# 16-bit lo squares from the third superblock on, in a convolution and squared-ReLU MLP kernel

## The chip, the cores and the metric

One core of one Trainium2 chip runs the kernel. The metric is the device time of one execution in microseconds (us), the median of several runs.

## What is computed

From the reference, cut:

```
# a causal convolution of 7 taps over the sequence, softmax taps, one set per head
w = exp(weight - max) / (sum + 1e-9)                  # 8 heads x 7 taps
out[b, s, h] = sum over k of w[h, k] * x[b, s + k - 6, h]   # x: 8 x 4096 x 192
# and a layer over its 32768 tokens of 192 channels
h = out @ w_in                                        # 192 x 2048
r = max(h, 0)
g = s * r * r + b
y = g @ w_out                                         # 2048 x 192
```

All inputs are 32-bit floats; the two weight matrices arrive as 64-bit words and each is kept as a hi and a lo part.

## The kernel before

Tokens lie along the free dimension. A superblock n is 1024 tokens (32 of them, NSUP), in two blocks j of 512; the 2048 hidden features are 8 pairs p of 256 (NPAIR). One **step** (n, j, p) is `first` (L702), the 18 matmuls of half height that give h for one pair; then on ScalarE `relu` and `square`; then the square is split into a hi part qh (a cast to fp32r, on ScalarE or VectorE) and a lo part ql = q - qh on VectorE; and `second` (L844), which multiplies qh by w_out's hi and lo parts and ql by w_out's hi part and adds into the block's accumulators. `second` runs two steps behind `first` (LAG, L28; three at a block's first pair), from a queue.

The lo part comes in two kinds, and SCALED (L34) says where the one gives way to the other. For superblocks n < SCALED, `lows` (L742) makes ql in 32 bits, and `second` runs 8 more half matmuls in each step for it (L854, operand ql). For n >= SCALED, `half_lows` (L769) makes ql in 16 bits into a ring of 26 places; the A columns of w_out (128 of the 192) are multiplied by all 8 pairs' ql at the block's end (L881), and the B columns (the other 64) for a batch of three blocks in one go (`lows_B`, L828), the earlier ones held until then (`holds`, L841). 16 bits need values of a known size, so for these superblocks the taps and weights are scaled by powers of two:
- `peak` (L227): VectorE finds the largest input of a superblock, SyncE's queue sends it to DRAM and reads it back to all partitions (`to_all`, L168). `scale` (L236) makes the scaled taps from it.
- `weight_tops` (L633): the maxima of the weights, a pair a step, during (SCALED - 1, 0); then `weight_peaks` (L645) sends them by POOL's queue to DRAM and back; `weight_scales` (L651) at (SCALED - 1, 1, 2) makes the scales.
- `halve` (L665): 16-bit copies of w_out in (SCALED, 0); `rescale` (L677): ScalarE scales w_out in place over 8 steps from (SCALED - 1, 1, 4) on.

`column_sums` (L608) adds up w_out over the hidden features, for the b term of g: on VectorE, a pair a step in (1, 1), and the four folds of the last lines at its end. `biases` (L686) uses them in (2, 0, 0).

The convolution of superblock n + 1 runs on VectorE beside the matmuls of n, in small parts: `convolve(k)` (L1003) draws k parts from the generator `Tokens.steps` (L340) of the next superblock. For superblock 1 (`steps_begin`, L345) these are 7 taps of A for block 0, 2 parts of its split, 7 taps of B, 2 parts of its split, 7 taps of A for block 1, 2 parts of its split. For later ones (`steps_by_block`, L355): 7 taps of B, a cast, then for each block 7 taps of A, the split of B, and two parts of the split of A: a copy on ScalarE, and the subtraction on VectorE, after which SyncE's queue issues the two swap DMAs of wA (L271, L272), a copy of sA with its halves exchanged. So a later superblock's first block is ready to use after 18 parts. A convolution's last tap ends a call early, except at p = 1, and what is left over is owed to the next call. BEGIN (L45) and PARTS (L39) say how many parts a step draws. `first` reads sA, then tB and wB, then wA.

What sets the order: each engine runs its own list of instructions in order, and so does each DMA queue (SyncE's SP queue, POOL's queue). The lists are made at build time by a scheduler that goes by the order of the code and by what is ready; `behind(engine)` (L140) keeps an instruction behind the last one of that engine in the code, `headed` (L1087) behind the head's last SyncE instruction, and the first superblock is kept in the order of the code (`in_order`, L144).

Of the kernel before, what the change touches and what calls it, by code (L numbers as in the profile page):

```python
# [9 lines left out]
F32 = mybir.dt.float32  # L10
# [8 lines left out]
P = 128  # L19
# [11 lines left out]
GAP = 128  # L31


SCALED = 3  # L34

RING = 26

# [5 lines left out]
)  # L43

BEGIN = {  # L45
    (1, 0): (3,) * 8,
    (1, 1): (1,) * 8,
# [4 lines left out]
}  # L52


# [8 lines left out]
def conv_attention_then_squared_relu_mlp(  # L63
# [137 lines left out]
    class Tokens:  # L201
# [34 lines left out]
        def scale(self):  # L236

            m = greatest(self.peaks, 1)
            v = small.tile([P, 3], F32, name="v", bufs=4)
            powers(m, v[:, 0:1], v[:, 1:2], -40)  # L240
            taps = small.tile([P, 2, K], F32, name="taps")
            nc.vector.tensor_scalar(
                taps, tap, v[:, 1:2], 2.0**3 if self.n == SCALED else c8,
                op0=ALU.mult, op1=ALU.mult,
            )
            self.tapA, self.tapB = taps[:, 0, :], taps[:, 1, :]
            self.v = v

        def unscale(self):

# [224 lines left out]
    def fetch(p, a=0, z=None):  # L475
        if a == 0:
            words[p] = wordp.tile([P, CT, 2], I32, name="words")
        z = z or CT
        nc.sync.dma_start(
            words[p][:, a:z].rearrange("p f w -> p (f w)"), w_words[p, :, 2 * a : 2 * z]  # L480
        )
# [126 lines left out]
    def column_sums(k):  # L608

        nonlocal sumA, sumB  # L610
        if k == 1:
            free = wordp.tile([P, CT, 2], I32, name="words").bitcast(F32)
            free = free.rearrange("p f w -> p (f w)")
            sumA = free[:, 0 : 4 * P].rearrange("p (h c) -> p h c", h=2)
            sumB = free[:, 4 * P : 4 * P + 5 * DB]
            nc.gpsimd.memset(sumB[:, 0:DB], 0.0)
        for o, w in (
            (sumA, W[:, k, :, CI:CB]),
            (sumB[:, DB:].rearrange("p (j d) -> p j d", j=2), WB[:, k, :, :]),
        ):  # L620
            before = W[:, 0, :, CI:CB] if o is sumA else WB[:, 0, :, :]
            before = before.bitcast(F32) if k == 1 else o
            nc.vector.tensor_tensor(o, before, w.bitcast(F32), op=ALU.add)
        if k == NPAIR - 1:
            a, b = sumA, sumB[:, DB:]
            nc.vector.tensor_tensor(a[:, 0, :], a[:, 0, :], a[:, 1, :], op=ALU.add)
            nc.vector.tensor_tensor(a[:, 0, 0:P], a[:, 0, 0:P], a[:, 0, P:], op=ALU.add)
            nc.vector.tensor_tensor(b[:, 0:P], b[:, 0:P], b[:, P:], op=ALU.add)
            nc.vector.tensor_tensor(b[:, 0:DB], b[:, 0:DB], b[:, DB:P], op=ALU.add)

# [99 lines left out]
    def squares(h, cast, scale=1.0):  # L730
        return square(relu(h, scale), cast)
# [37 lines left out]
    def half_lows(n, j, p, q, qh):  # L769


        k = ((n - SCALED) * 2 + j) * NPAIR + p
        ql = low_halves[n, j, p] = place(k % RING)
        nc.vector.tensor_tensor(  # L774
            ql.rearrange("p f (b a) -> p f b a", a=2),
            *(v.rearrange("p f (a b) -> p f b a", a=2) for v in (q, qh.bitcast(F32))),
            op=ALU.subtract,
        )
        return qh, ql
# [58 lines left out]

    held = []

    def holds(n, j):  # L841
        return n >= SCALED and (n, j) != steps[-1][:2] and (2 * (n - SCALED) + j) % BATCH < BATCH - 1

    def second(n, j, p, qh, ql):  # L844
        if (n, j, p) == steps[-1]:
# [157 lines left out]
    def convolve(k, stops=True):  # L1003


        k += owed[0]
        with behind(nc.vector, nc.scalar):
            while k and coming[0] in tok:
                try:
                    stop = next(tok[coming[0]].todo)  # L1010
                except StopIteration:
                    coming[0] += 1
                    continue
                k -= 1
                if stop and stops:
                    break
        owed[0] = k if coming[0] in tok else 0

    def pair(p):

        ha, hb = first(0, 0, p), first(0, 1, p)
        if p + 1 < NPAIR:
            if p not in TWICE:
                wide[p + 1].rest()
            ahead, between = 0, CONV[p] // 4
        else:
            ahead, between = CONV[p] // 2, CONV[p] // 4
        convolve(ahead)
        def magnitudes():
            if p + 2 < NPAIR:  # L1030
                wide[p + 2].magnitudes()

        if p + 1 in TWICE:
            return ahead_of_two(p, ha, hb, magnitudes)

        qa = relu(ha)
        if p in TWICE:
            qb = relu(hb)
            waiting.pop()()
            magnitudes()  # L1040
        qa = square(qa, nc.scalar.copy)
        if p not in TWICE:
            magnitudes()
        queue.append((0, 0, p, *lows(*qa)))
        if p + 2 < NPAIR:
            wide[p + 2].top()
        convolve(between)
        if p not in TWICE:
            qb = relu(hb)
        qb = square(qb, nc.scalar.copy)  # L1050
        if p + 2 < NPAIR:
            wide[p + 2].his()
        queue.append((0, 1, p, *lows(*qb)))
        convolve(CONV[p] - ahead - between)
# [29 lines left out]
    with in_order(nc.vector, nc.scalar, nc.tensor):  # L1084
        with in_order(nc.sync):
            head()
        headed = last_of(nc.sync)  # L1087
        for p in range(NPAIR):
            if p > 1:
                if p + 3 < NPAIR:  # L1090
                    with headed():
                        fetch(p + 3)
                pair(p)
            if p > 0 and p not in TWICE:
                while len(queue) > (LAG if p < NPAIR - 1 else 0):
                    second_whole(*queue.pop(0))
# [3 lines left out]
    for n, j, p in steps:  # L1100
        if p == 0:
            tok[n].finish(j)
            if j == 0:
                with headed():
                    start_tokens(n + 1)
            else:
                tok.pop(n - 1)
                if n >= SCALED:
                    with behind(nc.vector):
                        tok[n].unscale()  # L1110
                    tok_s[n] = tok[n].s
        if j == 1 and SCALED <= n + 2 < NSUP:
            if p == 0:
                load_tokens(n + 2)
            elif p == 5:
                with behind(nc.vector):
                    ahead[n + 2].peak()
        if n == SCALED - 1:
            if j == 0:
                with behind(nc.vector):  # L1120
                    weight_tops(p)
                    if p == NPAIR - 1:
                        wide_tops = weight_peaks()
            elif p == 2:
                with behind(nc.vector):
                    weight_scales(wide_tops)
        if (n, j) == (SCALED, 0):
            with behind(nc.vector):
                halve(p)
        if (n, j, p) in again:  # L1130
            with behind(nc.scalar):
                rescale(again[n, j, p])
        with begun() if n == 1 else ExitStack():
            h = first(n, j, p)
            if n < SCALED:
                on_scalar = (n, j) in ((1, 0), (2, 0)) or (n, j, p % 2) == (1, 1, 1)
                low = lows(*squares(h, nc.scalar.copy if on_scalar else nc.vector.tensor_copy))
            else:
                low = half_lows(n, j, p, *squares(h, nc.vector.tensor_copy, c if n == SCALED else 1.0))
            queue.append((n, j, p, *low))  # L1140
        if (j, p) == (0, 1) and SCALED <= n + 1 < NSUP:
            with behind(nc.vector):
                tok[n + 1].scale()
        if (n, j) == (1, 1):
            if p < NPAIR - 1:
                with behind(nc.vector):
                    column_sums(p + 1)
        if (n, j) in BEGIN:
            convolve(BEGIN[n, j][p], p != 1)
        else:  # L1150
            batched = (2 * (n - SCALED) + j) % BATCH == 0
            convolve(PARTS[batched][j][p], p != 1)
        if (n, j, p) == (2, 0, 0):
            biases()


        while queue and len(queue) > LAG + (queue[0][2] == 0 and queue[0][:2] != (1, 0)):
            item = queue.pop(0)
            (second if item[0] else second_whole)(*item)
# [47 lines left out]
```

## Time and profile before

| what | value |
|---|---|
| median of 3 runs | 2039.15 us (2037.92 to 2039.29) |
| the profiled execution | 2037.69 us |
| its span, first to last instruction | 2035.9 us |
| granted TensorE clock, mean | 1.000 |
| chain that ended last | TensorE 96%, VectorE 3% |

The span lacks the start and end of the execution, 1.8 us. Busy shares are shares of the span. The matmuls overlap (two of half height run beside each other), so a matmul's own duration says little; the distance from one group's start to the next group's is what it costs.

### The profile page before, as it was taken

The page shows a single profiled execution, that of the slowest core. Times are in us where ns is not written, and L with a number is a line of the kernel's source. Part 1 is how long each engine was busy: PE and PEld are TensorE (multiplying, and loading weights), DVE is VectorE, ACT ScalarE, POOL GpSimd, SP SyncE. Part 2 cuts the span into 40 slices and gives each one's busy share as a digit, 9 for nine tenths or more (in the row PEclk, how much of TensorE's full clock was granted, in tenths as well). Part 3 has the DMA queues.
Part 4 walks back from the last instruction along what each step waited for, and adds up shares of the span by engine and source line. Part 5 has one row for each costly group of instructions (what it writes and reads, how often), then busy time and mean ns, then how long its engine had stood idle before and what let it go on. Part 6 is the DMA issues. An engine that isn't in the chain of part 4 may idle for free.

```text
span 2035.9 us, 43199 instructions
## 1 busy us (share of the span) xinstructions
PE 2026.6 (100%) x18404; PEld 1643.4 (81%) x18404; DVE 1692.0 (83%) x2340; ACT 1324.1 (65%) x1444; POOL 242.5 (12%) x319
## 2 busy tenths in 40 slices
PE   9999999999999999999999999999999999999999
PEld 6889987877878887878778788888787787888886
DVE  9888897888888888878788888878787888888874
ACT  8878766656666565666656666656666666656564
POOL 0001101010110101010101111010101011110101
PEclk9999999999999999999999999999999999999999
DMA  5013333242332332332424323323324243232221
GB/s 197 21 45 92 81 81 80 52 94 60 87 78 68 80 81 66 80 76 55 95 56 91 75 66 84 76 71 76 76 58 97 56 92 73 61 91 66 61 63 40
DMA packets 74625, 152.83 MB, mean 75 GB/s; under 512 B 19040, under 2 KB 23008, under 8 KB 74432
## 3 DMA queue, kind: packets, MB, share of 16 engines
q1 hardware_dynamic: 44448, 86.87, 16.3%
q0 software_dynamic: 29840, 63.07, 14.9%
q8 instruction: 144, 2.36, 0.6%
q14 instruction: 49, 0.40, 0.1%
q10 hardware_dynamic: 144, 0.13, 0.0%
HBM read 35.57 MB, written 25.20 MB: 30 GB/s over the span
## 4 chain that ended last, share of the span: by engine, by line
PE 96%; DVE 3%; issue 0%; DMA 0%; SPq 0%; DVEq 0%
PE h L711 48%; PE acc L854 33%; PE acc L881 10%; PE h L834 3%; PE acc L834 2%; DVE ql L744 1%; DVE c L452 0%; DVE t L438 0%; DVE accA L263 0%; DVE t L435 0%; DVE W L460 0%; DVE W L458 0%; DVE c L451 0%; DVE t L431 0%; PE acc L794 0%
## 5 line engine op out<-in xcount | busy, mean ns | idle before, releaser
L727 ACT ACTIVATE q<-h 128x1024 f32<-128x1024 f32 x492 | 502.7, 1022 | 492.1 <-PE h L711 492.1
L739 DVE CAST qh<-q 128x1024 fp32r<-128x1024 f32 x477 | 330.9, 694 | 288.5 <-ACT q L734 287.5
L734 ACT ACTIVATE q<-q 128x1024 f32<-128x1024 f32 x508 | 539.6, 1062 | 14.1
L854 PE MATMUL acc<-qh,W 64*128 64x512 f32 x3960 | 510.7, 376 | 0.0
L711 PE MATMUL h<-sA,W 64*128 64x512 f32 x3072 | 430.2, 384 | 3.5 <-DVE W L460 1.9
L854 PEld LDWEIGHTS acc<-qh,W 64*128 64x128 f32 x3960 | 379.0, 186 | 50.2
L711 PE MATMUL h<-wA,W 64*128 64x512 f32 x3072 | 417.9, 376 | 0.0
L711 PE MATMUL h<-tB,W 64*128 64x512 f32 x1536 | 413.6, 376 | 0.0
L711 PE MATMUL h<-wB,W 64*128 64x512 f32 x1536 | 413.6, 376 | 0.0
L711 PEld LDWEIGHTS h<-sA,W 64*128 64x128 f32 x3072 | 293.9, 186 | 51.9 <-DVE W L460 2.6
L711 PEld LDWEIGHTS h<-wA,W 64*128 64x128 f32 x3072 | 294.5, 186 | 39.1
L711 PEld LDWEIGHTS h<-tB,W 64*128 64x128 f32 x1536 | 283.7, 186 | 26.0 <-issue 0.2
L854 PE MATMUL acc<-qh,WB 64*128 64x512 f32 x1980 | 297.1, 376 | 0.0
L711 PEld LDWEIGHTS h<-wB,W 64*128 64x128 f32 x1536 | 283.7, 186 | 13.0
L263 DVE SCALAR_TENSOR_TENSOR accA<-xA,taps,accA 128x512 f32<-128x512 f32 x348 | 260.1, 748 | 3.1
L774 DVE TENSOR_TENSOR ql<-q,qh 128x1024 f16<-128x1024 f32 x180 | 226.9, 1261 | 6.2
L854 PEld LDWEIGHTS acc<-qh,WB 64*128 64x128 f32 x1980 | 190.1, 186 | 25.4 <-DVE qh L739 0.4
L774 DVE TENSOR_TENSOR more<-q,qh 128x1024 f16<-128x1024 f32 x140 | 176.5, 1261 | 4.8
L881 PEld LDWEIGHTS <-words 64*128 64x128 f16 x1852 | 85.5, 94 | 113.2 <-issue 17.3
L910 POOL DMA_DIRECT2D oB<-oB x60 | 58.0, 967 | 745.0 <-ACT oB L898 715.4
L774 DVE TENSOR_TENSOR words<-q,qh 128x1024 f16<-128x1024 f32 x108 | 136.2, 1261 | 3.7
L263 DVE SCALAR_TENSOR_TENSOR accB<-xB,taps,accB 128x512 f32<-128x512 f32 x174 | 130.2, 748 | 1.5
(182 smaller groups left out, 1611.4 us busy)
## 6 DMA issues: line engine op xcount, KB each, us to landing
wA<-sA SPq DMA_DIRECT2D x126, 256.0 KB, 4.3
wB<-tB SPq DMA_DIRECT2D x124, 128.0 KB, 2.9
oB<-oB POOLq DMA_DIRECT2D x60, 256.0 KB, 3.5
oA<-oA POOLq DMA_DIRECT2D x60, 256.0 KB, 3.8
outT<-oA POOLq DMA_DIRECT2D x60, 256.0 KB, 2.3
xA<-in_xA SPq DMA_DIRECT2D x24, 515.0 KB, 3.6
xB<-in_xB SPq DMA_DIRECT2D x32, 259.0 KB, 2.6
oB<-oB POOLq DMA_DIRECT2D x60, 128.0 KB, 3.7
```

The costliest lines, as they stand in the source:

```text
L263: nc.vector.scalar_tensor_tensor(acc, src, w[:, k : k + 1], acc, op0=ALU.mult, op1=ALU.add)
L711: nc.tensor.matmul(h[:, i, :], w_in(w, p, chunk[0], rows), folded(chunk[part]), start=start, stop=stop,)
L727: nc.scalar.activation(q, h, AF.Relu, scale=scale)
L734: nc.scalar.activation(q, q, AF.Square)
L739: cast(qh, q)
L744: nc.vector.tensor_tensor(ql, q, qh.bitcast(F32), op=ALU.subtract)
L774: nc.vector.tensor_tensor(ql.rearrange("p f (b a) -> p f b a", a=2), *(v.rearrange("p f (a b) -> p f b a", a=2) for v in (q, qh.bitcast(F3 ...
L834: nc.tensor.matmul(to[k * DB :][0:DB], halves[1][:, 2 * p + k, :], ql[:, k, :], start=start and p == 0, stop=p == NPAIR - 1, skip_group_ch ...
L854: nc.tensor.matmul(accs[to + 2 * i], w(f, r), folded(q[r, f % 2, :]), start=start and f == 0, stop=stop and f == ends[i],)
L881: nc.tensor.matmul(accs[2 * i], halves[0][r, f, :], low[r], start=False, stop=f == ends[i],)
L910: nc.gpsimd.dma_start(o[1], o[3], accum_op=ALU.add)
```

## The change

SCALED goes from 3 to 2: superblock 2 has 16-bit lo squares as well. What hangs on SCALED moves with it: `weight_tops` to (1, 0), `weight_scales` to (1, 1, 2), `rescale` to (1, 1, 4) and on, `halve` to (2, 0). The peak of superblock 2 is taken in (1, 0, 0), its scale in (1, 0, 5), and its convolution can't begin before that (`ready`). `column_sums` becomes DMAs on POOL's queue, the first a copy, the other seven accumulating, a pair a step in (1, 0) by the code; the folds are `fold_sums`, in (1, 1, 3). BEGIN has new numbers. Batches are counted from the end, so the first one is of two blocks. Casts of qh: ScalarE takes all of (1, 0), p < 4 of (1, 1), and p > 4 of (2, 0); VectorE the others.

```diff
-SCALED = 3
+SCALED = 2
 BEGIN = {
-    (1, 0): (3,) * 8,
-    (1, 1): (1,) * 8,
-    (2, 0): (2, 2, 2, 2, 2, 2, 2, 1),
-    (2, 1): (2, 3, 2, 2, 1, 0, 1, 2),
-    (3, 0): (2, 2, 2, 2, 2, 2, 2, 1),
-    (3, 1): (2, 4, 2, 1, 1, 0, 1, 2),
+    (1, 0): (0, 2, 2, 2, 2, 1, 2, 2),
+    (1, 1): (3, 3, 2, 2, 2, 1, 2, 2),
+    (2, 0): (2, 2, 2, 2, 2, 2, 2, 3),
+    (2, 1): (2, 4, 2, 1, 1, 0, 1, 2),
 }
+        def ready(self):
+            return self.n < SCALED or hasattr(self, "v")
     def column_sums(k):
-        if k == 1:
+        if k == 0:
...
+        how = {"accum_op": ALU.add} if k else {}
         for o, w in (
             (sumA, W[:, k, :, CI:CB]),
             (sumB[:, DB:].rearrange("p (j d) -> p j d", j=2), WB[:, k, :, :]),
         ):
-            before = W[:, 0, :, CI:CB] if o is sumA else WB[:, 0, :, :]
-            before = before.bitcast(F32) if k == 1 else o
-            nc.vector.tensor_tensor(o, before, w.bitcast(F32), op=ALU.add)
-        if k == NPAIR - 1:
-            ...
+            nc.gpsimd.dma_start(o, w.bitcast(F32), **how)
+    def fold_sums():
+        ...
+    def left(n, j):
+        return 2 * (NSUP - 1 - n) - j
     def holds(n, j):
-        return n >= SCALED and (n, j) != steps[-1][:2] and (2 * (n - SCALED) + j) % BATCH < BATCH - 1
+        return n >= SCALED and (n, j) != steps[-1][:2] and left(n, j) % BATCH > 0
     # convolve
-            while k and coming[0] in tok:
+            while k and coming[0] in tok and tok[coming[0]].ready():
     # the head's loop over p
+                if p == 5:
+                    with headed():
+                        load_tokens(SCALED)
     # the loop over steps
+        if (n, j, p) == (SCALED - 1, 0, 0):
+            with behind(nc.vector):
+                tok[SCALED].peak()
             if n < SCALED:
-                on_scalar = (n, j) in ((1, 0), (2, 0)) or (n, j, p % 2) == (1, 1, 1)
+                on_scalar = j == 0 or p < 4
...
-                low = half_lows(n, j, p, *squares(h, nc.vector.tensor_copy, c if n == SCALED else 1.0))
+                cast = nc.scalar.copy if (n, j) == (SCALED, 0) and p > 4 else nc.vector.tensor_copy
+                low = half_lows(n, j, p, *squares(h, cast, c if n == SCALED else 1.0))
-        if (j, p) == (0, 1) and SCALED <= n + 1 < NSUP:
+        if (j, p) == (0, 5 if n < SCALED else 1) and SCALED <= n + 1 < NSUP:
             with behind(nc.vector):
                 tok[n + 1].scale()
-        if (n, j) == (1, 1):
-            if p < NPAIR - 1:
-                with behind(nc.vector):
-                    column_sums(p + 1)
+        if (n, j) == (1, 0):
+            column_sums(p)
+        if (n, j, p) == (1, 1, 3):
+            with behind(nc.vector):
+                fold_sums()
-            batched = (2 * (n - SCALED) + j) % BATCH == 0
+            batched = left(n, j) % BATCH == BATCH - 1
```

## Rows read from the trace of the kernel before

A timeline's columns are the start in us, the us from there to the group's end, the engine (SPq is SyncE's DMA queue), the line, the operation, out<-in, the number of instructions merged, and in brackets the idle time before it with what ended it.

**Rows 1.** The page's first part (busy us, share of the span, number of instructions) and the granted clock in 40 slices of the span, in tenths.

```profile
PE 2026.6 (100%) x18404; PEld 1643.4 (81%) x18404; DVE 1692.0 (83%) x2340; ACT 1324.1 (65%) x1444; POOL 242.5 (12%) x319
...
PEclk9999999999999999999999999999999999999999
```

**Rows 2.** What TensorE's matmuls waited for, over the whole span (us in total, times, longest), and the last such wait in TensorE's timeline.

```profile
PE h L711 <- DVE W L460: 1.9, 1, 1.9
...
71.99 0.48 PE L711 MATMUL h<-sA,W 64*128 64x512 f32 x2 [0.19 <-DVE W L466]
```

**Rows 3.** TensorE's timeline in superblock 1: the start of first(1,1,0) and its reading of wA, the start of the next step, the lo squares of second(1,1,2), the start of first(2,0,0), its reading of wB and of wA.

```profile
119.54 0.81 PE L711 MATMUL h<-sA,W 64*128 64x512 f32 x6
...
120.83 0.81 PE L711 MATMUL h<-wA,W 64*128 64x512 f32 x6
...
123.64 0.81 PE L711 MATMUL h<-sA,W 64*128 64x512 f32 x6
...
139.18 0.60 PE L854 MATMUL acc<-ql,WB 64*128 64x512 f32 x4
...
152.34 0.81 PE L711 MATMUL h<-sA,W 64*128 64x512 f32 x6
...
153.64 0.81 PE L711 MATMUL h<-wA,W 64*128 64x512 f32 x6
```

**Rows 4.** TensorE's timeline with 16-bit lo squares: the end of block (3,0) with its A columns' group (L881) and the next step, two successive steps of (3,1), and the first rows of the B columns' groups of the first and the second batch of three blocks (L834).

```profile
252.87 3.63 PE L881 MATMUL acc<-ql,words 64*128 64x512 f16 x32
256.15 1.00 PE L711 MATMUL h<-sA,W 64*128 64x512 f32 x6
...
269.28 0.81 PE L711 MATMUL h<-sA,W 64*128 64x512 f32 x6
...
272.52 0.81 PE L711 MATMUL h<-sA,W 64*128 64x512 f32 x6
...
311.70 2.35 PE L834 MATMUL h<-ql,words 128*64 128x512 f16 x20
...
405.19 0.62 PE L834 MATMUL h<-more,words 128*64 128x512 f16 x4
```

**Rows 5.** VectorE's timeline in (2,0): from the weight maxima of one step to those of the next, with a lo square and two taps between.

```profile
170.52 0.87 DVE L640 TENSOR_REDUCE tops<-W 128x1 f32<-128x384 f32 x2
...
174.09 0.87 DVE L640 TENSOR_REDUCE tops<-W 128x1 f32<-128x384 f32 x2
```

**Rows 6.** The way of the weights' maxima in VectorE's timeline (both_tops; and m, the first instruction of the scales, behind two DMAs on POOL's queue) and POOL's timeline: the memset of the column sums' buffer and the next thing POOL did.

```profile
185.74 0.29 DVE L648 TENSOR_REDUCE both_tops<-tops 128x1 f32<-128x8 f32 x2
...
199.99 0.42 DVE L185 TENSOR_REDUCE m<-t 128x2 f32<-128x256 f32 x1 [1.63 <-DMA t<-there]
...
52.90 0.15 POOL L616 MEMSET words<- 128x64 f32 x1 [51.41 <-DVE c L452]
130.76 1.57 POOL L902 TENSOR_TENSOR oB<-oB,oB 128x512 f32<-128x512 f32 x1 [77.70 <-ACT oB L898]
```

**Rows 7.** ScalarE's timeline: the cast of (1,0,5), the relus of (1,0,7) and (1,1,1), and the square of (1,1,6).

```profile
111.99 1.05 ACT L739 CAST qh<-q 128x1024 fp32r<-128x1024 f32 x1
...
117.58 1.02 ACT L727 ACTIVATE q<-h 128x1024 f32<-128x1024 f32 x1 [0.90 <-PE h L711]
...
125.79 1.02 ACT L727 ACTIVATE q<-h 128x1024 f32<-128x1024 f32 x1 [1.98 <-PE h L711]
...
147.35 1.07 ACT L734 ACTIVATE q<-q 128x1024 f32<-128x1024 f32 x1
```

**Rows 8.** The accumulating DMAs of the outputs on POOL, whole span: duration of one on POOL in ns (min, median, max), and from the view of the same line the us from issue to landing.

```profile
L910 POOL DMA_DIRECT2D oB<-oB x60: 843/857/1341, 164.3 to 2001.1; - x60
...
DMA to landing us min/median/max: 3.1/3.5/6.4
```

**Rows 9.** VectorE's timeline from the lo squares of (1,0,0) to the next ones.

```profile
96.43 1.23 DVE L744 TENSOR_TENSOR ql<-q,qh 128x1024 fp32r<-128x1024 f32 x1 [2.82 <-ACT qh L739]
97.69 0.69 DVE L312 TENSOR_TENSOR tB<-accB,hiB 64x512 fp32r<-64x512 f32 x1
98.41 0.49 DVE L261 TENSOR_SCALAR accA<-xA,tap 128x512 f32<-128x512 f32 x1
98.93 1.54 DVE L263 SCALAR_TENSOR_TENSOR accA<-xA,tap,accA 128x512 f32<-128x512 f32 x2
```

**Rows 10.** SyncE's queue in (1,1): the second of the two swap DMAs of wA for (2,0,0), the peak of superblock 3 on its way out and back; and from the view of tile wA from 100 to 160 us the time of the swaps from issue to landing.

```profile
139.23 0.59 SPq L272 DMA_DIRECT2D wA<-sA  x1
146.33 0.39 SPq L171 DMA_DIRECT2D there<-peak  x1
154.14 0.34 SPq L177 DMA_DIRECT2D t<-there  x1
...
DMA to landing us min/median/max: 3.0/3.6/3.7
```

**Rows 11.** VectorE's timeline: the first bias addition and the lo squares of (2,0,0), the cast of (3,0,7); and TensorE's first use of the latter.

```profile
156.41 0.15 DVE L694 TENSOR_TENSOR bias<-bias,h 128x2 f32<-128x2 f32 x1
...
158.76 1.21 DVE L744 TENSOR_TENSOR ql<-q,qh 128x1024 fp32r<-128x1024 f32 x1
...
250.45 0.69 DVE L739 CAST qh<-q 128x1024 fp32r<-128x1024 f32 x1
...
251.57 0.59 PE L854 MATMUL acc<-qh,WB 64*128 64x512 f32 x4
```

More of the change, by code (lines that the diff above doesn't have):

```diff
@@ L620, in column_sums @@
         ):
-            before = W[:, 0, :, CI:CB] if o is sumA else WB[:, 0, :, :]
-            before = before.bitcast(F32) if k == 1 else o
-            nc.vector.tensor_tensor(o, before, w.bitcast(F32), op=ALU.add)
-        if k == NPAIR - 1:
[L625 to L629, printed above, removed]
+            nc.gpsimd.dma_start(o, w.bitcast(F32), **how)
+    def fold_sums():
+        a, b = sumA, sumB[:, DB:]
+        nc.vector.tensor_tensor(a[:, 0, :], a[:, 0, :], a[:, 1, :], op=ALU.add)
+        nc.vector.tensor_tensor(a[:, 0, 0:P], a[:, 0, 0:P], a[:, 0, P:], op=ALU.add)
+        nc.vector.tensor_tensor(b[:, 0:P], b[:, 0:P], b[:, P:], op=ALU.add)
+        nc.vector.tensor_tensor(b[:, 0:DB], b[:, 0:DB], b[:, DB:P], op=ALU.add)
     def weight_tops(p):
```

## The prediction

> **What bounds the kernel now.** I read the share of busy time first [rows 1]: TensorE is busy for 2026.6 of 2035.9 us, the next engine for 83%, and the granted clock is at its full level in all slices. Then who TensorE waited for [rows 2]: a few waits, the longest 1.9 us, the last of them at 71.99 us. So from there on the matmuls follow each other without a gap, and the time is their number times their pitch. Any saving must be fewer or shorter matmuls, and any loss must be a new hole between them. Third, the pitch itself, from TensorE's timeline. With 32-bit lo squares a step (one pair p of one block) takes 123.64 - 119.54 = 4.10 us, and the block from (1,1,0) to (2,0,0) takes 152.34 - 119.54 = 32.80 us [rows 3]. With 16-bit lo squares a step takes 272.52 - 269.28 = 3.24 us; the lo squares come at the block's end in 3.28 us for the A columns (252.87 to 256.15) and, once for each batch of three blocks, for the B columns. Three such blocks, from one batch's B group to the next, take 405.19 - 311.70 = 93.49 us, which is 31.16 a block [rows 4].
>
> **The change, part by part.**
>
> The gain. Superblock 2 has two blocks that go from 32.80 to 31.16 us: 2 x 1.64 = 3.3 us less on the engine that is the bound. The first batch is now of two blocks, not three. That changes no count of matmuls, since each block's B group is 16 of them wherever it stands. No other matmul goes away.
>
> Maxima and scales one half to one superblock sooner. weight_tops and the peak of token 2 go to (1,0). A step there is then on VectorE the weight maxima, one lo square and two taps of the convolution, which is what superblock 2 holds in the trace: 174.09 - 170.52 = 3.57 us [rows 5], below TensorE's 4.10. Cost 0: at the start of (1,0) VectorE isn't late, it stood 2.82 us for ScalarE [rows 9], which the new peak and maxima fill. The scales themselves: from both_tops (185.74) to the scales' first instruction (199.99) two POOL DMAs and their landings lie, 14.25 us, and VectorE stood 1.63 us before it [rows 6]. Now both_tops comes in (1,0,7), whose relu is at 117.58 [rows 7], so at about 121, and the scales at about 135.3. VectorE gets to that place, the start of (1,1,2), at about 131.5 (relu of (1,1,1) at 125.79 [rows 7], 3.1 for it, square and cast, 1.2 for the subtraction, 1.5 for its steps) and stands nearly 4 us, with the lo squares of (1,1,2) queued behind it. They end 2.2 us after the scales begin (1.0 for the scales, 1.2 for the subtraction), at 137.5. TensorE reads them from second(1,1,2) at 139.18 on [rows 3]. Cost 0, with 1.7 us to spare. The cover is the two steps by which second runs behind first.
>
> The column sums leave VectorE (14 additions on an engine that isn't the bound, worth 0) and become 16 POOL DMAs, each behind the landing of the one before on the same tile. The nearest row is the accumulating DMA of the outputs: 0.86 us of issue, 3.5 us to landing, 6.4 at most [rows 8]. Eight rounds of 4.4 us are 35 us. POOL reached the memset of the same buffer at 52.90 in the old kernel [rows 6], though its place in the code is in (1,1), and POOL has nothing else until 130.76, so I expect the sums to run from 53 to about 88, beside the first superblock's matmuls. With 7.7 us a round they end at 115, still ahead of both_tops at 121. Cost 0; bounds 0 to the rival below.
>
> The Trainium skill speaks against this part: "SBUF — State Buffer", section "SBUF: two separate sides", says that a DMA issued from POOL waits for its descriptors while VectorE holds the port that the two share, and gives 620 ns that became 3100. The trace has these DMAs beside a VectorE that is 83% busy and shows 6.4 us at worst against 3.1 at best, so about twice, not five times. By five times the sums would take 124 us and the case is the last rival; by the row they cost nothing.
>
> Less head start for the convolution. This is the part that costs. BEGIN gives 13 steps in (1,0), where it gave 24, since VectorE has the maxima to do, and token 2 can't start before its scale in (1,0,5). One step is left over from the head: between the lo squares of (1,0,0) at 96.43 and the next ones the trace shows four steps (a split and three taps) where BEGIN says three [rows 9].
> - Token 1's second block then needs 10 steps and has 1, 3, 5, 7, 8 and 10 after (1,0,0) to (1,0,5) (the end of a convolution stops a step). Its last one, the subtraction and the swap DMAs of wA, stands behind the lo squares and the scale of (1,0,5): the cast of that step ends at 113.04 [rows 7], then 1.2 for the subtraction, 1.1 for the scale, 0.7 for the split, so the swaps are issued at 116.2 and 116.7. With 3.6 us to landing [rows 10] that is 120.3; first(1,1,0) reads wA at 120.83 [rows 3]. VectorE may be up to 1 us behind this. Cost 0 to 0.6; I take 0.2.
> - Token 2 must have 18 steps done for (2,0,0). It has 4 after (1,0) and gets 3, 3, 2, 2, then 1, 2 and 1, so step 18 falls in (1,1,6). In the old kernel its second swap was issued at 139.23 [rows 10], 14 us before its use. Now: the square of (1,1,6) ends at 148.42 [rows 7], the cast (VectorE from p = 4 on) at 149.1, the lo squares at 150.3, the split at 151.0; swaps at 151.1 and 151.6, landed at 155.2. TensorE wants wA at 153.64 [rows 3]. It is 1.6 us late. If VectorE carries on its 4 us wait from the scales it is up to 3.2. If the scheduler puts second(1,1,6), whose inputs are there, ahead of the waiting matmuls, nothing is lost: it does reorder by readiness, since the bias additions at 156.41 ran ahead of the lo squares at 158.76, which stand first in the code [rows 11]. I take 1.6, the sum from rows without lag; ends 0 and 3.2.
>
> Superblock 2 with the 16-bit work. VectorE was tight there in superblock 3: the cast of (3,0,7) ended at 251.14, and TensorE's first use is at 251.57 [rows 11]. The new one adds the bias additions (156.41 to 158.76, 2.4 us) and takes away three casts (p = 5 to 7 of (2,0) on ScalarE, 3 x 0.7 = 2.1). Cost 0 to 0.5, taken as 0. Loading token 2 at p = 5 of the head changes no landing that anything waits for: 0.
>
> **The sum** for the profiled execution: 2037.69 (span 2035.9 and 1.8 around it) - 3.3 + 0.2 + 1.6 = 2036.2. The profiled execution stands 1.46 below the median of the three runs, so the same change to the median gives 2039.15 - 1.5 = 2037.6. A measurement of this kernel can tell about 0.2%, 4.1 us, from no change. The whole gain is 3.3, so even without a loss this change stays below that.
>
> **The rivals.**
> - Nothing is late: the swaps are covered, by reordering or since landing is quicker (3.0 us was seen at best). 2039.15 - 3.3 = 2035.8. For it: second is there to fill the hole. Against it: the chain for (2,0,0) is 1.6 us short even at the trace's own pace.
> - SyncE's queue turns the late swap into a long one, and it is slower than before. In (1,1,5) the peak of token 3 is sent out and read back: the first DMA was issued at 146.33, and the second could go only at 154.14, as it waits for the first to land [rows 10]. In the old kernel no swap fell between. Now the swaps of tB (about 150) and of wA (151) do. If the read-back stands ahead of them in the queue, they go at 154.5 to 156.1 and wA lands near 159.7, 6 us after 153.64; with VectorE 1 us late it is 7. Net -3.3 + 0.2 + 6 to 7 = +2.9 to +3.9, 2042.0 to 2043.1, and a further 1 us of lag makes it slower by over 0.2%. It decides on one thing: whether the read-back or the swap is put first.
> - POOL is late with the column sums and holds the weights' maxima behind them: either since the sums are not placed early, or since their landing stretches. Each us after 121 + 1.7 holds the scales, VectorE and then second(1,1,2). Sums that began only in (1,0), at 93, would end near 128, which is 5 us of wait, 2039.15 - 1.5 + 5 = 2042.7, and from 129 on it is slower by over 0.2%. Against it: the memset at 52.90. The second of the two ways is what the Trainium skill's section above would give; no row here shows it.
> - The change does save the matmuls, as every term of n >= SCALED follows the constant; that it does nothing can be left out.
>
> **How the numbers follow.** The forecast (part of the gain lost in (2,0,0)) has 0.42, nothing late 0.25, SyncE's queue 0.2, POOL late 0.05, other lags of VectorE in (2,0) 0.08. Range: the low end is the whole gain and the runs' scatter of 1.2 below their median, 2034.8; the high end is the middle of SyncE's case, 2042.6. Faster by over 0.2% needs more than the whole gain, only scatter in the second case gives it: 0.07. Slower by over 0.2%: the upper third of SyncE's case and most of POOL's, 0.13. Within 0.2%: 0.80.
>
> **What would show it.** Right: the pitch of the steps in superblock 2 is 3.24 us with 16-bit groups at the blocks' ends; its two blocks take about 62.4 us in place of 65.6; TensorE waits once at (2,0,0) for wA, 1 to 3 us, released by a SyncE DMA; the column sums' DMAs stand between 53 and 90 us. Wrong: a wait of 5 us or more at (2,0,0) with the read-back of the peak ahead of the swaps (second rival), POOL's first maxima DMA after 125 us (third), no wait at all (first), or a wait of second on qh or ql in (1,1,2) or at the end of (2,0).

## The result, and the profile after

The changed kernel takes 2051.77 us (median of 6 runs, 2050.48 to 2052.28), the kernel before 2037.96 beside it (6 runs, 2037.79 to 2039.29). The ratio is 1.0065, 95% interval 1.0052 to 1.0078: slower by 13.8 us, where 1.5 less was forecast. The profiled execution took 2050.55 us, its span is 2048.8, so 12.9 over that of before. In some executions (traced in e2_fill, e3_begun, e4_all and e6_scales_step3 below) TensorE's granted clock stands at half its level for some 3.3 us behind 49 us, so that all that follows in them is 1.2 to 1.7 us later, and the medians below hold executions of both kinds.

The shares of busy time and the granted clock, which answer to [rows 1]: TensorE is busy 1.7 us more than before in a span 12.9 longer, and the clock, which was full in every slice, falls in the fourth (154 to 205 us).

```profile
PE 2028.3 (99%) x18372; PEld 1631.9 (80%) x18372; DVE 1692.6 (83%) x2341; ACT 1317.5 (64%) x1439; POOL 255.7 (12%) x335
PEclk9998999999999999999999999999999999999999
```

TensorE's waits (engine, what it works on, who released it: total, times, longest). Against [rows 2] there is a new one of 7.3 us on wB, one of 1.3 on sA, and ScalarE's q has one of 1.5.

```profile
PE h L713 <- DMA wB<-tB: 7.3, 1, 7.3
PE h L713 <- ACT q L729: 2.6, 3, 1.5
PE h L713 <- DVE W L461: 1.9, 1, 1.9
PE h L713 <- DVE sA L281: 1.3, 1, 1.3
```

TensorE's timeline where [rows 3] had superblock 1 (start, duration, instruction, the wait before it). The first line is first(1,0,2), which waits for the relu of (1,0,0); the others are (2,0,0) up to the first matmul of (2,0,1).

```profile
96.86 0.92 PE L713 MATMUL h<-sA,W 64*128 64x512 f32 x6 [1.47 <-ACT q L729]
...
154.60 0.48 PE L713 MATMUL h<-sA,W 64*128 64x512 f32 x2
156.34 0.70 PE L713 MATMUL h<-sA,W 64*128 64x512 f32 x4 [1.26 <-DVE sA L281]
...
164.53 1.34 PE L713 MATMUL h<-wB,W 64*128 64x512 f32 x2 [7.28 <-DMA wB<-tB]
...
167.34 1.64 PE L713 MATMUL h<-wA,W 64*128 64x512 f32 x5 [0.23 <-DMA wA<-sA]
...
172.47 1.02 PE L713 MATMUL h<-sA,W 64*128 64x512 f32 x6
```

SyncE's queue in the same stretch, the rows that answer to [rows 10]. The read-back (t<-there) waits for the first DMA to land, and the four swaps of token 2 go out in the 2.2 us behind it. VectorE had written tB at 153.63 and sA at 156.28 (the second fence has its row), so the swaps of wB stood ready for 5.5 us and those of wA for 4.1. That is the second rival's order.

```profile
150.68 0.38 SPq L169 DMA_DIRECT2D there<-peak  x1
158.68 0.33 SPq L175 DMA_DIRECT2D t<-there  x1
159.12 0.47 SPq L273 DMA_DIRECT2D wB<-tB  x1
...
160.92 0.59 SPq L273 DMA_DIRECT2D wA<-sA  x1
```

```profile
155.60 0.68 DVE L281 TENSOR_TENSOR sA<-accA,sA 128x512 fp32r<-128x512 f32 x1
```

The profile's chain of work that ended last takes the same way (start, us, what); from 148.92 to the matmuls it is VectorE's maximum, the two DMAs and the swap:

```profile
148.92 1.74 DVE peak L229 x2
150.68 7.94 DMA there<-peak
158.68 0.33 SPq L175
...
160.92 6.38 DMA wA<-sA
167.34 1.23 PE h L713 x5
```

The DMA issues from 140 to 172 us (KB each, median us to landing). The swaps of wA, which landed in 3.0 to 3.7 us in the kernel before [rows 10], take 6.1 here, where all four go out within 2.2 us and the read-back's own 128 KB just ahead of them; those of wB take 5.4. In e1_peak_early below, where they go two and two, it is 3.4 and 2.2.

```profile
wA<-sA SPq DMA_DIRECT2D x2, 256.0 KB, 6.1
wB<-tB SPq DMA_DIRECT2D x2, 128.0 KB, 5.4
```

Windows over the hole (window, its length, busy time and instructions of the five engines, then the granted clock, the DMA share, GB/s). The clock stands at 2.4 GHz until TensorE has stopped, and at 1.2 GHz from 158 to 170 us, so part of the matmuls behind the hole run at half speed.

```profile
154.00:158.00 4.00, 1.99 (x15) 1.16 (x12) 3.79 (x6) 1.57 (x2) 0.00 (x0) 0.97 0.00 0
158.00:162.00 4.00, 0.00 (x0) 0.00 (x0) 2.37 (x5) 0.00 (x0) 0.00 (x0) 0.50 0.05 3
162.00:166.00 4.00, 1.47 (x5) 0.79 (x5) 0.00 (x0) 0.00 (x0) 0.00 (x0) 0.50 0.99 218
166.00:170.00 4.00, 3.75 (x19) 2.75 (x19) 0.00 (x0) 0.93 (x1) 0.00 (x0) 0.50 0.04 8
```

**Where the 12.9 us are.** (2,0,0) begins at 154.60, before at 152.34: +2.26. Of these 0.30 are there already at 91 us, 1.63 come with the late relu of (1,0,0), and 0.33 one step on, where the weights' sequencer waits 0.36 us for that step's qh; from 101.29 on (before 99.03) nothing is added. From there to (2,0,1) it takes 17.87 us, before 4.55 (152.34 to 156.89): +13.32. From (2,0,1) on nothing is late and the gain comes: the B group of the batch of (3,0) to (4,0) starts at 323.91, before at 311.70 [rows 4], so of +15.58 there are +12.21 left. That is 3.37 gained, forecast 3.3. The difference stays at 12.2 up to the last matmuls; the last 0.7 is the landing of the last output DMA, 4.07 us from issue to the end of the span against 3.38 before. Of the seven edits of the changed kernel below, with the same code there, it is 4.01 to 4.07 in five, 3.63 in e4_all and 3.33 in e5_pool_queue; why, no run here shows.

The 13.32 split in two. With its operands there, the last group of wA (x5) is followed by the next step after 3.14 us (158.28 to 161.42 in e1_peak_early, full clock). Here it is 167.34 to 172.47, so 5.13: 2.0 us are the clock, and 11.3 are wA's lateness.

### The profile page after: what moved, and what is told of

Same layout as the page of the kernel before. It is cut to its first block, busy times and chain, and to the rows that moved or that the text cites. A ratio compares the mean times of both kernels' runs of the same rounds, so it can differ in the third digit from the quotient of the medians.

```text
span 2048.8 us, 43132 instructions
## 1 busy us (share of the span) xinstructions
PE 2028.3 (99%) x18372; PEld 1631.9 (80%) x18372; DVE 1692.6 (83%) x2341; ACT 1317.5 (64%) x1439; POOL 255.7 (12%) x335
## 4 chain that ended last, share of the span: by engine, by line
PE 94%; DVE 4%; DMA 1%; ACT 0%; issue 0%; SPq 0%; DVEq 0%; ACTq 0%
PE h L713 47%; PE acc L859 32%; PE acc L886 10%; PE h L836 3%; PE acc L836 2%; DVE ql L746 1%; DVE accA L264 0%; DVE c L453 0%; DMA there<-peak 0%; DVE t L439 0%; DMA wA<-sA 0%; DVE t L436 0%; DVE W L461 0%; DVE W L459 0%; DVE c L452 0%
## 5 line engine op out<-in xcount | busy, mean ns | idle before, releaser
L264 DVE SCALAR_TENSOR_TENSOR accA<-xA,taps,accA 128x512 f32<-128x512 f32 x360 | 268.8, 747 | 3.3
L776 DVE TENSOR_TENSOR ql<-q,qh 128x1024 f16<-128x1024 f32 x190 | 239.4, 1260 | 6.4
L776 DVE TENSOR_TENSOR more<-q,qh 128x1024 f16<-128x1024 f32 x144 | 181.4, 1260 | 4.9
L264 DVE SCALAR_TENSOR_TENSOR accB<-xB,taps,accB 128x512 f32<-128x512 f32 x180 | 134.4, 747 | 1.6
```

The lines of the kernel that those rows point to most:

```text
L264: nc.vector.scalar_tensor_tensor(acc, src, w[:, k : k + 1], acc, op0=ALU.mult, op1=ALU.add)
L776: nc.vector.tensor_tensor(ql.rearrange("p f (b a) -> p f b a", a=2), *(v.rearrange("p f (a b) -> p f b a", a=2) for v in (q, qh.bitcast(F3 ...
```

## The experiments

Theory (from the trace): the hole is a queue. The swaps stand behind the read-back of token 3's peak on SyncE, VectorE's lag makes that later, and the clock adds to it. Each experiment is an edit of the changed kernel, if nothing else is said. In these runs the kernel before took 2038.76 (e1 to e4) and 2038.32 us (e5 to e8).

**e1_peak_early**: token 3's peak is taken and sent three steps sooner, so the read-back lies far ahead of the swaps.

```
-            elif p == 5:
+            elif p == (2 if n == 1 else 5):
                 with behind(nc.vector):
                     ahead[n + 2].peak()
```

> Against 2051.8 of the changed kernel. Queue theory: the read-back of superblock 3's peak no longer stands in front of the swaps for (2,0,0), so they go when VectorE is done, near 153.5 to 155, and land near 158; the hole before (2,0,0) shrinks from 8.8 to about 2.5 us, the granted clock stays at its full level, and the time falls by 6 plus the 4.5 of the half-clock stretch, to about 2041. Late-convolution theory: the swaps are late by VectorE's own lag whatever the queue does; a hole of over 5 us and a drop of the clock stay, 2046 or more.

Measured: 2041.67 us, ratio 1.0015 [1.0006, 1.0024]; 10 of the 13.8 us are back. SyncE's queue and TensorE's waits:

```profile
137.49 0.38 SPq L169 DMA_DIRECT2D there<-peak  x1
145.23 0.33 SPq L175 DMA_DIRECT2D t<-there  x1
...
154.05 0.46 SPq L272 DMA_DIRECT2D wA<-sA  x1
154.56 0.59 SPq L273 DMA_DIRECT2D wA<-sA  x1
```

```profile
157.19 0.48 PE L713 MATMUL h<-wA,W 64*128 64x512 f32 x1 [1.34 <-DMA wA<-sA]
158.28 0.91 PE L713 MATMUL h<-wA,W 64*128 64x512 f32 x5 [0.60 <-DMA wA<-sA]
```

The swaps land 3.1 and 3.7 us after issue, and TensorE stands 1.94 us for them. That is the size of the forecast's own term (1.6, 0 to 3.2). But the edit does two things: it clears the queue, and it takes the peak's two reductions (1.22 and 0.68 us) off VectorE's way to the split, which ends at 153.90 in place of 156.28. The traced execution took 2039.48 us, the lowest of ten that reach 2043.53, so what the others lost more is not shown.

**e5_pool_queue**: the edit of e1 moves work on VectorE too. This one changes the queue alone and leaves the peak where it is.

```
-            self.peaks = to_all(m, nc.sync)
+            self.peaks = to_all(m, nc.gpsimd if self.n == 3 else nc.sync)
```

> The changed kernel, with one thing different: the two DMAs that send token 3's peak out and read it back are issued from POOL, not SyncE. VectorE's order and its lag stay. Queue theory: the four swaps of token 2 no longer stand behind the read-back, they go out as soon as VectorE has written what they copy: tB's at about 153.7, wA's behind the split (155.60) at 156.3 and 156.8. With a landing of 3 to 3.7 us wA is there at 160 to 160.5 in place of 167.3, TensorE waits some 4 to 5 us, and about 3 us later (5 with half clock) it starts (2,0,1): 163.4 to 165.4, where the changed kernel has 172.47. That is 7 to 9 us back: 2042.7 to 2044.7 us. Rival, VectorE's lag alone: nothing comes back, 2051 to 2052. Second rival, four swaps are slow in any queue (6 to 7 us to landing): wA at 163.5, 2046 to 2048.

Measured: 2044.47 us, ratio 1.0031 [1.0019, 1.0043]. The swaps go out at 152.14 and 155.60, while the read-back on POOL still waits until 158.57:

```profile
155.60 0.46 SPq L272 DMA_DIRECT2D wA<-sA  x1
156.11 0.59 SPq L273 DMA_DIRECT2D wA<-sA  x1
```

```profile
158.52 0.81 PE L713 MATMUL h<-wB,W 64*128 64x512 f32 x2 [2.10 <-DMA wB<-tB]
...
161.22 1.65 PE L713 MATMUL h<-wA,W 64*128 64x512 f32 x5 [1.47 <-DMA wA<-sA]
...
167.10 1.02 PE L713 MATMUL h<-sA,W 64*128 64x512 f32 x6
```

That is 7.3 us of the median and 6.1 between the traced executions, of which 0.7 is the landing at the end. (2,0,0) takes 12.46 us (154.64 to 167.10) for 17.87, so 5.4 less, and up to 0.8 of these are VectorE: the split begins at 154.76 here, as the maxima of the weights landed sooner (8.0 us for 10.9). So the queue is worth 4.6 to 5.4 us of the step, and 7.9 over the 4.55 of before remain without it. (2,0,1) comes later than the 163.4 to 165.4 expected, since wA landed 0.7 us later (5.1 us behind its issue) and the clock cost 2.7 (5.88 us from wA's last group, for 3.14). wB, issued on time at 152.14, took 6.2 us to land; why, no run here shows.

**e6_scales_step3**: the scales one step later, so that VectorE doesn't stand 3.97 us for them.

```
-            elif p == 2:
+            elif p == 3:
                 with behind(nc.vector):
                     weight_scales(wide_tops)
```

> The changed kernel, with the scales of the weights computed in step (1,1,3), not (1,1,2). VectorE then has the lo squares and taps of a further step to do before it comes to the wait of 3.97 us for the scales' maxima, so it stands under 1 us. If the lag of VectorE at the end of (1,1) is that wait carried on, the peak of token 3 goes out about 3 us sooner (147.5 in place of 150.7), and with the read-back the swaps: wA lands near 164, 3 us sooner. Queue theory (the read-back, not VectorE, holds the swaps): the hole is 3 us shorter and no more, about 2048.5 us. Rival, the lag of VectorE is what makes the swaps late: with the split at about 152.5 wA lands at 156.5, the hole is under 2 us and the time 2041 or so. Rival, the lag is not from the scales: no change, 2051 to 2052.

Measured: 2050.78 us, ratio 1.0060 [1.0045, 1.0075]. The wait is gone, but the peak is sent at 150.53, 5.3 us ahead of (2,0,0) in place of 3.9, so only 1.4 us were won. VectorE in (1,1,2), with POOL's additions beside it:

```profile
134.07 1.50 DVE L262 TENSOR_SCALAR accA<-xA,taps 128x512 f32<-128x512 f32 x1
135.61 1.65 DVE L264 SCALAR_TENSOR_TENSOR accA<-xA,taps,accA 128x512 f32<-128x512 f32 x1
```

```profile
133.81 1.48 POOL L907 TENSOR_TENSOR oB<-oB,oB 128x512 f32<-128x512 f32 x1 [0.30 <-ACT oB L903]
135.26 1.45 POOL L910 TENSOR_TENSOR oA<-oA,oA 128x512 f32<-128x512 f32 x1
```

These taps take 0.48 and 0.75 us in the changed kernel, and a third addition of POOL makes two more taps 1.03 us longer, so 2.95 of the 3.97 us are lost again: in the changed kernel the two additions shown fall into VectorE's wait. So the edit took away 1.4 us of lag, not 3. The hole follows it: wA's last group begins 10.61 us behind the start of (2,0,0) (155.83 to 166.44), for 12.74, but the half clock behind it cost 3.0 us, for 2.0, so the step takes 16.75 us (to 172.58) for 17.87, and the median is 1.0 lower. The swaps still stand behind the read-back: tB was written at 153.48 and its swaps go at 158.82. What the time would be with no lag of VectorE at all, this run does not show.

**e2_fill**: the first group of first(2,0,0) is repeated 11 times, so that TensorE has matmuls in the hole (each repeat starts the sum anew).

```
-        for at in (0, 2, 1):
+        for k, at in enumerate((0,) * again + (0, 2, 1)):
...
-            both(1, 1, at, False, at == 1)
+            both(1, 1, at, False, at == 1 or k < again)
...
-            h = first(n, j, p)
+            h = first(n, j, p, again=11 if (n, j, p) == (2, 0, 0) else 0)
```

> In (2,0,0) the first group of matmuls is run 11 times more (7.1 us of TensorE work that changes nothing), so TensorE works where it stood waiting for tB and wB. Clock theory: the hole's length stays but the granted clock stays at its full level after it; the 4.5 us of the half-clock stretch are saved and the time falls to about 2047.3, although more matmuls run. If the clock is no part of the loss: no gain, 2051.8 or up to 2 us more.

Measured: 2051.16 us, ratio 1.0061, so 0.6 us of the expected 4.5. The clock held through the fill and still fell at 169 us, behind a wait of 1.46 us for wA:

```profile
156.13 8.40 PE L713 MATMUL h<-sA,W 64*128 64x512 f32 x72
...
168.04 0.91 PE L713 MATMUL h<-wA,W 64*128 64x512 f32 x5 [1.46 <-DMA wA<-sA]
...
172.87 1.01 PE L713 MATMUL h<-sA,W 64*128 64x512 f32 x6
```

From wA to the next step it is 4.83 us, for 5.13 in the changed kernel, so this run does not show what a full clock behind the hole saves. By the 3.14 us of e1_peak_early it is 2.0, not the expectation's 4.5: most of the half-clock time lies within the wait for wA and costs nothing of its own.

**e3_begun**: the peak of token 2 and the weight maxima of (1,0) also wait, in the order of the program, for the end of superblock 0, so that VectorE first evacuates it (moves its accumulators out to oA and oB).

```
-            with behind(nc.vector):
+            with begun(), behind(nc.vector):
                 tok[SCALED].peak()
...
-                with behind(nc.vector):
+                with begun(), behind(nc.vector):
                     weight_tops(p)
```

> Only the order on VectorE at (1,0,0): the peak of superblock 2 and the first weight maxima come behind the last evacuation of superblock 0, not ahead of it. If the 1.5 us wait of first(1,0,2) for the relu is from that order, that wait is gone and VectorE is 2 us earlier through (1,0), so everything up to (2,0,0) moves by 1.5 to 2.5 us, to about 2050. If the hole at (2,0,0) is set by something that does not move with VectorE, the hole takes it up: 2051.8.

Measured: 2047.86 us, ratio 1.0044, so 3.9 us less than the changed kernel. The wait of 1.47 us is gone, and first(1,0,2) and first(1,0,3) follow at the distances of before (94.72, 96.67, 100.77 on TensorE, so 1.95 and 4.10 us). The hole stays, with 6.37 us for wB in place of 7.28: the peak goes out 1.8 us sooner (148.89), and (2,0,0) takes 15.91 us (154.08 to 169.99) for 17.87, so 2.0 more are won there, which the expectation didn't have.

**e4_all**: e1, e3 and two more steps of convolution in (1,1,1), BEGIN[(1, 1)] = (3, 5, 2, 2, 2, 1, 2, 2), so that the swaps are sent in time.

> The peak of superblock 3 at (1,1,2), the order at (1,0,0) of the run before, and two more parts of the convolution in (1,1,1), so that the swaps for (2,0,0) go two steps sooner. If the loss is all in the waits up to (2,0,0) and their half-clock stretch: no wait of TensorE after 72 us, and the gain of the matmuls alone is left, 2038.0 - 3.3 = 2034.7. If the column sums' DMAs, the batch of two or the heavier superblock 2 cost something as well: 2036 or more, with waits of second or longer steps in (2,0).

Measured: 2038.08 us, ratio 0.9998 [0.9989, 1.0006]. No wait is left at (2,0,0) (154.17 to 158.72, 4.55 us), but of the gain 2 us were missing. From (2,0,0) to the B group of the batch of (3,0) it won 1.39 us, not 3.37. ScalarE at the end of (2,0,1), and TensorE's sequencer of weights:

```profile
162.01 1.06 ACT L736 ACTIVATE q<-q 128x1024 f32<-128x1024 f32 x1
164.75 0.62 ACT L279 CAST sA<-accA 128x512 fp32r<-128x512 f32 x1 [1.68 <-DVE accA L264]
165.28 0.77 ACT L900 ACTIVATE oB<-acc,bias,sb 128x512 f32<-128x512 f32 x1
```

```profile
167.34 0.18 PEld L859 LDWEIGHTS acc<-qh,W 64*128 64x128 f32 x1 [0.37 <-ACT oA L900]
...
167.92 0.73 PEld L859 LDWEIGHTS acc<-qh,W 64*128 64x128 f32 x7 [0.40 <-ACT oA L903]
```

The split's cast L279 now stands ahead of the evacuation of (1,1) on ScalarE, which it does not in the changed kernel; it waits for VectorE's taps, and TensorE gets its accumulators late. The same comes at (2,1,1), with a wait of 3.55 us.

**e7_split_apart**: e4 with two steps fewer in (2,0,1).

```
-    (2, 0): (2, 2, 2, 2, 2, 2, 2, 3),
+    (2, 0): (2, 0, 2, 2, 2, 2, 2, 3),
```

> The kernel of e4_all with BEGIN[(2, 0)] = (2, 0, 2, 2, 2, 2, 2, 3), so two steps of convolution fewer in (2,0,1). In e4_all ScalarE's cast of the split (sA from accA) stood ahead of the evacuation of (1,1) and of (2,0), and ScalarE stood there 1.68 and 3.55 us for VectorE's taps; TensorE then got its accumulators late, 0.67 and 0.87 us, and 0.43 us more went at steps between. Theory: with the cast behind the evacuation in both blocks these 1.97 us come back: 2038.1 - 2.0 = 2036.1 us, below the kernel before by 2 to 3 us (ratio 0.9988). Rival, the gain of the 16-bit squares is smaller than 3.4 us and the evacuation costs nothing: 2038, the same as the kernel before. Rival, the two steps are missing later: a wait for wA in (2,1,0), 2038 to 2040.

Measured: 2036.19 us (11 runs, 2034.99 to 2036.70), ratio 0.9988 [0.9979, 0.9996]: below both kernels, by little. (2,0,0) starts at 152.56, and the B group of the batch of (3,0) at 308.34, 3.36 us ahead of [rows 4]; from the one to the other it won 3.58, where e4_all won 1.39, so the whole gain is there. In the time 2.1 of it are left by the medians and 2.7 between the traced executions, since the last output DMA lands later here too (4.04 us, for 3.38). The waits of TensorE are those of before; the two longest:

```profile
PE h L713 <- DVE W L461: 1.9, 1, 1.9
PE h L713 <- ACT q L729: 1.1, 2, 0.6
```

**e8_sums_only**: the kernel before with the column sums by DMA and nothing else of the change.

```
-            before = W[:, 0, :, CI:CB] if o is sumA else WB[:, 0, :, :]
...
+            nc.gpsimd.dma_start(o, w.bitcast(F32), **how)
...
+        if (n, j) == (1, 0):
+            column_sums(p)
+        if (n, j, p) == (1, 1, 3):
+            with behind(nc.vector):
+                fold_sums()
```

> The kernel before, with the column sums alone taken over from the changed one: 16 accumulating DMAs of POOL in place of VectorE's 14 additions, the fold in (1,1,3). SCALED stays 3 and the convolution's steps stay. Theory: cost 0 and gain 0, since VectorE is not the bound in the first superblock nor in (1,1), and the DMAs run from 53 to 88 us beside matmuls: within 0.5 us of the kernel before, 2038.5 or so. Rival: the DMAs and VectorE get in each other's way (SBUF, or the port of POOL and VectorE), VectorE's instructions between 53 and 88 us get longer, and the relu of (1,0,0) or the lo squares come late: 1 to 3 us slower, with a new wait of TensorE at about 95 us.

Measured: 2038.18 us, ratio 1.0000 [0.9991, 1.0009]. No new wait at 95 us, and the time is the same within 0.1%.

## Why the prediction was wrong, point by point

- **The bound, and the gain**: right. 3.37 us forecast as 3.3, steps of 3.24 us in superblock 2 (186.28, 189.52, 192.75 on TensorE), and e7_split_apart has it whole on TensorE.
- **Column sums**: right, where and at what price. The sums were issued from 53.76 to 83 us in rounds of about 4 us, and e8_sums_only costs nothing that can be told. First and last DMA on POOL in the changed kernel:

```profile
53.76 0.88 POOL L623 DMA_DIRECT2D words<-W  x1 [0.40 <-issue]
...
81.63 1.38 POOL L623 DMA_DIRECT2D words<-WB  x1
```

  An issue took 1.4 us at most, for the 0.86 of [rows 8], and a landing 3.6 (7.7 at most). The five-fold of the Trainium skill ("SBUF — State Buffer", "SBUF: two separate sides") was not met here.
- **Maxima in (1,0), "cost 0"**: wrong. The prediction read VectorE's idle 2.82 us behind qh [rows 9] as room. But the scheduler put the new peak and maxima ahead of the evacuation of superblock 0, which ScalarE's relu of (1,0,0) waits for: idle time later in the step doesn't help what stands ahead of it. It cost 1.96 us (1.63 and 0.33), and in e3_begun both are gone. VectorE in the changed kernel:

```profile
90.88 1.21 DVE L229 TENSOR_REDUCE peak<-xA 128x1 f32<-128x1030 f32 x1
...
92.61 0.86 DVE L642 TENSOR_REDUCE tops<-W 128x1 f32<-128x384 f32 x2
...
93.59 0.73 DVE L811 TENSOR_SCALAR oA<-acc,sb 128x512 f32<-128x512 f32 x1
```

- **Scales, "cost 0, with 1.7 us to spare"**: right for TensorE in (1,1,2), and VectorE did stand 3.97 us. That length belongs to this trace in part: the DMA that sends the maxima out took 10.9 us to land in this trace and 7.8 to 8.1 in e1_peak_early, e3_begun, e5_pool_queue and e6_scales_step3, and in e3 and e5, where the scales' place is the same, VectorE stood 0.87 and 1.17 us. Of what it carried to the end of (1,1), e6_scales_step3 won back 1.4 us.
- **Swap for (1,1,0), 0.2**: 0. It went out 2.7 us later than worked out (118.87), but TensorE was 2.3 us later too, and first(1,1,0) reads wA at 123.09, 1.30 behind its start as before.
- **Swap for (2,0,0), 1.6 late**: the step that failed. wA was to have landed at 155.2, and it landed at 167.3, 12.1 us later. Of these, 5.3 lie ahead of the swap: sA was written at 156.28, worked out was 151.0, 2.26 for TensorE's own lateness and 3.0 for VectorE's lag behind it. 4.0 are the queue: the second swap went out 4.6 us behind the split, worked out was 0.6. 2.8 are the landing, 6.4 us for 3.6. The likeliest case had no read-back ahead of the swaps; that order was given 0.2. And the chain of (1,1,6) took VectorE as free behind ScalarE's square: it had no term for the peak's two reductions (148.83 to 150.65), which come ahead of the split there. So the term doesn't hold with the queue free alone: in e5_pool_queue wA's last group begins 6.58 us behind the start of (2,0,0), before 1.30, which is 5.3 late and outside 0 to 3.2. Only where the reductions are gone as well (e1_peak_early) is the wait 1.94.
- **The second rival's price**, net 2.9 to 3.9, was wrong too. It had wA land at 159.7; it landed at about 167.3, since the peak was sent at 150.68 and not at 146.33 (4.35: TensorE's own 2.26 and some 2 of VectorE), the read-back took 0.2 longer, the swaps behind it went out 0.3 later, and with four of them sent together the last of wA took 6.4 us to land (160.92 to 167.3), not 3.6. And no term stood for the clock, 2.0 us.
- **Superblock 2, "0 to 0.5"**: 0. Nothing is late there in the changed kernel, and in e1_peak_early, with little of the hole left, (2,0,1) to the B group takes as long (161.42 to 312.86, 151.44 us). It cost 2 us only in e4_all, by where the split falls, and nothing in e7_split_apart.
- **Range**: missed at the high end (2042.6) by 9 us. The bounds of the late swap's cost were taken from rows of a TensorE without a hole; for one with a hole it needed the clock and the four landings, and for VectorE what else stands ahead of the split.

## What to carry to other kernels

A DMA that waits for another one to land holds all that stands behind it in its queue: before moving work towards such a pair, write out that queue with issue times, and give the round trip (8 us here) a queue of its own or a place far ahead of what is urgent. An engine's idle time in a step is room only for what stands behind the urgent instruction, so ask for each added one what it is put ahead of, and of a chain over two engines what else the second one does in between. And price a new hole on TensorE with what follows it: operands that were sent together landed later (5.4 to 6.4 us here, for 3.0 to 3.7), and the matmuls behind the hole ran at half clock.

## What the runs showed of the hardware

- The granted clock fell to 1.2 GHz in the hole of 7.3 us and was still there when the matmuls came back, which cost 2.0 us behind the wait (2.2 in e3_begun, 3.0 in e6_scales_step3); with holes of 2.1 and 1.5 us near each other (e5_pool_queue) it fell too and cost 2.7; with 1.34 and 0.60 (the traced execution of e1_peak_early) it did not. Matmuls in the hole kept it full (e2_fill, until 169 us), but it fell behind a further wait of 1.46 us.
- The 1-KB DMA that sends the peak out took 7.9 us to land (7.4 to 8.0 in the other runs), and 8.2 from POOL's queue. That of the weights' maxima, from POOL, took 7.7 to 8.5 us in nine traces and 10.9 in that of the changed kernel; why, no run here shows.
- VectorE's taps take 1.50 and 1.65 us beside POOL's additions, for 0.48 and 0.75. The Trainium skill ("SBUF — State Buffer", "SBUF: two separate sides") has the two engines share a pair of ports which one instruction holds for its whole length; these rows agree: the first tap ends 0.28 us and the second 0.55 us behind the end of the POOL addition beside it, each 0.2 us less than it takes alone, so more than half of each tap lies behind that end.
